# Linformer attention and a gelu MLP on one core: scores, sums and values in 64x32 tiles of TensorE, one round of sums per block, reciprocals copied to the heads' rows through DRAM

## Chip, cores and metric

One core of a Trainium2 chip. The metric is the time of one execution on the device in microseconds (us), the median of repeated executions. Most executions of a kernel agree within 0.3%.

## The reference

```python
# batch 8, heads 8, seq 1024, head_dim 64, k_proj 64; d_model 512, d_ff 2048; float32
k_proj = np.einsum('ks,bhsd->bhkd', E, k)
v_proj = np.einsum('ks,bhsd->bhkd', F, v)
scores = np.matmul(q, k_proj.transpose(0, 1, 3, 2)) / 8
attn = np.exp(scores - scores.max(-1, keepdims=True))
attn = attn / (attn.sum(-1, keepdims=True) + 1e-09)
x = np.matmul(attn, v_proj)            # -> [8192 tokens, 512]
h = x @ w_in                           # [8192, 2048]
out = (h / (1 + np.exp(-1.702 * h))) @ w_out
```

## The kernel before

The 8192 tokens are worked in 16 blocks of 512 (two blocks per batch). Each block j goes through ffn1 (16 slots of four matmuls) and ffn2 (eight slots O to O+7 of eight matmuls). The attention of later blocks is put between these slots with `at(block, slot, ...)`. A block's attention is scores, exp on ScalarE, then `norm`: sums of the exponentials over the 64 keys, values, reciprocal, product. A head has 64 keys and 64 columns, so each matmul is a 64x64 tile and four run in the array side by side.

```python
def four(outs, lhsTs, rhss):
    for i, ro in ((0, (LO, HI)), (1, (HI, LO))):
        for ri, r in zip((LO, HI), ro):
            nc.tensor.matmul(outs[i][r], lhsTs[i][ri], rhss[i][ri], start=True, stop=True)

def norm(h, u):                      # heads 4u .. 4u+3 of block h
    def go():
        e = [expT[h][:, 2 * u + i, :] for i in range(2)]
        d_ps = [ps_d.tile([P, TB], F32, name="d_ps") for _ in range(2)]
        four(d_ps, [ones, ones], e)                      # sums, already on the heads' rows
        n_ps = [ps_n.tile([P, TB], F32, name="n_ps") for _ in range(2)]
        four(n_ps, [vqs[h // NB2 % 2][:, 2 * u + i, :] for i in range(2)], e)
        for i in range(2):
            rden = att.tile([P, TB], F32, name="rden")
            nc.vector.reciprocal(rden, d_ps[i])
            nc.vector.tensor_tensor(x_of(h)[:, 2 * u + i, :], n_ps[i], rden, op=ALU.mult)
    return go
```

`ps_n` and `ps_d` have two PSUM buffers each, `ps_f` four: all eight banks are taken. Loads of q, k and v go on GpSimd's queue; outputs and the DMA transposes of q (`q_dma`) and of the projected k (in `kv_out`) go on the SP queue, in program order. In the schedule (cut):

```python
at(1, O + 7, q_dma(2))
at(2, 1, norm(3, 0)); at(2, 11, norm(3, 1))
at(2, 2, proj(2)); at(2, 3, kv_out(2))
for b in range(3, B):
    j = NB2 * b - 4
    at(j, O, q_dma(b)); at(j, O + 6, proj(b), kv_out(b))
at(2, O + 5, norm(4, 0)); at(3, 4, norm(4, 1))
for j in range(3, NBLK - 2):
    for u in range(2):
        at(j, O + 6 * u, scores(j + 3, u)); at(j, O + 6 * u, norm(j + 2, u))   # [cut]
```

The softmax here doesn't subtract the row's maximum and nothing guards it: scores larger than these inputs give would overflow.

Of the kernel before, what the change touches and what calls it, by code (L numbers as in the profile page):

```python
# [9 lines left out]
F32 = mybir.dt.float32  # L10
BF16 = mybir.dt.bfloat16
AF = mybir.ActivationFunctionType
ALU = mybir.AluOpType
# [4 lines left out]
def kernel(ctx, tc, q, k, v, E, F,  # L18
                                                     moe_w_in, moe_w_out, out):
    nc = tc.nc  # L20
    B, H, S, D = q.shape
    KP, _ = E.shape
    DM, DFF = moe_w_in.shape
    P = 128
    J = S // P
    NB2 = S // 512
    HP = H // 2
    KC = DM // P
    FC = DFF // P
    TB = 512  # L30
    JB = TB // P
    NBLK = B * S // TB
# [3 lines left out]
    consts = ctx.enter_context(tc.tile_pool(name="consts", bufs=1))  # L36
    ldpool = ctx.enter_context(tc.tile_pool(name="ldpool", bufs=1))
    att = ctx.enter_context(tc.tile_pool(name="att", bufs=2))
    work = ctx.enter_context(tc.tile_pool(name="work", bufs=2))
    ps_f = ctx.enter_context(tc.tile_pool(name="ps_f", bufs=4, space=PSUM))  # L40
    ps_d = ctx.enter_context(tc.tile_pool(name="ps_d", bufs=2, space=PSUM))
    ps_n = ctx.enter_context(tc.tile_pool(name="ps_n", bufs=2, space=PSUM))
    ctx.enter_context(tc.manual_schedule())


# [54 lines left out]
    LO, HI = slice(0, KP), slice(KP, P)  # L100
    X_LO, X_HI = slice(0, None, 3), slice(1, 3)
    kts = [consts.tile([P, HP, KP], BF16, name=f"kt{i}") for i in range(2)]
    vqs = [consts.tile([P, HP, D], BF16, name=f"vq{i}") for i in range(2)]
    zeros = consts.tile([P, TB], BF16)
    nc.vector.memset(zeros, 0.0)
    ones = consts.tile([P, D], BF16)
    nc.vector.memset(ones, 1.0)

    vxs = []
# [7 lines left out]
    def f_tile(shape, dt=F32):  # L117
        return ps_f.tile(shape, dt, name="f_ps")
# [15 lines left out]
    warm(4)  # L134


    kvps, kbs, qT, expT, xT = {}, {}, {}, {}, {}

    def proj(b):
        def go():  # L140
            kvps[b] = f_tile([P, H, D])
            for j in range(J):
                for e, r in enumerate((LO, HI)):
                    nc.tensor.matmul(kvps[b][r], eft[:, j, e * KP:(e + 1) * KP],  # L144
                                     (kt, vt)[e][b][:, :, j, :],
                                     start=(j == 0), stop=(j == J - 1))
        return go
# [21 lines left out]
    def v_out(b, v_ps, p0, n, cp=nc.vector.tensor_copy):  # L169
        if b < 2:  # L170
            if n == 1:
                for r, t in ((LO, p0 % 2), (HI, 1 - p0 % 2)):
                    cp(vxs[b][r, 2 * p0 + t, :D], v_ps[HI, t, :])
            else:
                vv = v_ps[HI].rearrange("k (u x) d -> k u x d", x=4)
                vx = vxs[b][:, 2 * p0:2 * (p0 + n), :D].rearrange("k (u x) d -> k u x d", x=4)
                for r, xs_ in ((LO, X_LO), (HI, X_HI)):
                    cp(vx[r, :, xs_], vv[:, :, xs_])
        if b > 0:
            vv = v_ps[HI].rearrange("k (u x) d -> k u x d", x=4)  # L180
            for r, xs_ in ((LO, X_LO), (HI, X_HI)):
                nc.vector.tensor_copy(vqs[b % 2][r].rearrange("k (u e) d -> k u e d", e=2), vv[:, :, xs_, :])

    def kv_out(b):
        def go():
            ps = kvps.pop(b)
            k_b = att.tile([KP, H, D], BF16, name="k_b")
            nc.vector.tensor_copy(k_b, ps[LO])  # L188
            if b > 1:
                nc.sync.dma_start_transpose(out=kts[b % 2], in_=k_b.rearrange("k h d -> k (h d)"))  # L190
            v_out(b, ps, 0, HP)
            kbs[b] = k_b
        return go
# [13 lines left out]
    def q_dma(b, j0=0, n=J):  # L207
        def go():
            if j0 == 0:
                qT[b] = att.tile([P, J, HP, P], BF16, name="qT")  # L210
            nc.sync.dma_start_transpose(out=qT[b][:, j0:j0 + n].rearrange("r j p s -> r (j p) s"),
                                        in_=qt[b][:, j0:j0 + n].rearrange("s j h d -> s (j h d)"))
        return go

    def four(outs, lhsTs, rhss):

        for i, ro in ((0, (LO, HI)), (1, (HI, LO))):
            for ri, r in zip((LO, HI), ro):
                nc.tensor.matmul(outs[i][r], lhsTs[i][ri], rhss[i][ri], start=True, stop=True)  # L219

    def scores(h, u, half=None):
        b, c = divmod(h, NB2)
        j0, n = (c * JB, JB) if half is None else (c * JB + half * JB // 2, JB // 2)
        ts = slice(j0 * P - c * TB, (j0 + n) * P - c * TB)

        def go():
            if h not in expT:
                expT[h] = att.tile([P, HP, TB], BF16, name="expT", bufs=3)
            s_ps = [f_tile([P, n * P]) for _ in range(2)]
            four(s_ps, [kts[b % 2][:, 2 * u + i, :] for i in range(2)],  # L230
                 [qT[b][:, j0:j0 + n, 2 * u + i, :] for i in range(2)])
            for i in range(2):
                nc.scalar.activation(expT[h][:, 2 * u + i, ts], s_ps[i], AF.Exp, scale=scale)  # L233
        return go
# [4 lines left out]
    def x_of(h):  # L239
        if h not in xT:  # L240
            xT[h] = att.tile([P, KC, TB], BF16, name="xT", bufs=3)
        return xT[h]

    def norm(h, u):
        def go():
            e = [expT[h][:, 2 * u + i, :] for i in range(2)]
            d_ps = [ps_d.tile([P, TB], F32, name="d_ps") for _ in range(2)]
            four(d_ps, [ones, ones], e)
            n_ps = [ps_n.tile([P, TB], F32, name="n_ps") for _ in range(2)]
            four(n_ps, [vqs[h // NB2 % 2][:, 2 * u + i, :] for i in range(2)], e)  # L250
            for i in range(2):
                rden = att.tile([P, TB], F32, name="rden")
                nc.vector.reciprocal(rden, d_ps[i])  # L253
                nc.vector.tensor_tensor(x_of(h)[:, 2 * u + i, :], n_ps[i], rden, op=ALU.mult)  # L254
        return go


# [18 lines left out]
    def x_tr(h, p, half):  # L276
        def go():
            x_sb = xs.pop((h, p, half)).rearrange("s (i t) d -> s i (t d)", i=2)
            n_ps = ps_n.tile([P, 2, P], BF16, name="n_ps")
            for i in range(2):  # L280
                nc.tensor.transpose(n_ps[:, i, :], x_sb[:, i, :], ident)  # L281
            cp = nc.scalar.copy if (h, half) == (0, 0) else nc.vector.tensor_copy
            cp(x_of(h)[:, p, half * TB // 2:(half + 1) * TB // 2], n_ps.rearrange("r i s -> r (i s)"))
        return go
# [53 lines left out]
    def at(j, slot, *fs):  # L338
        fill.setdefault((j, slot), []).extend(fs)

    O = FC
# [40 lines left out]
    for u in range(2):  # L382
        at(1, O + u, scores(2, u))
        at(1, O + 3 + u, scores(3, u))
        at(2, O + 2 * u, scores(4, u))
        at(2, O + 3 + 2 * u, scores(5, u))
    for p in range(HP):
        at(1, O + 2 + p, tok(2, p, 0), tok(2, p, 1))
        at(1, O + 3 + p, x_tr(2, p, 0), x_tr(2, p, 1))
    at(2, 1, norm(3, 0))  # L390
    at(2, 11, norm(3, 1))
    for j in (1, 2):
        at(j, O + 5, gelu_table)
    at(1, O + 7, q_dma(2))
    at(2, 2, proj(2))
    at(2, 3, kv_out(2))
    for b in range(3, B):
        j = NB2 * b - 4
        at(j, O, q_dma(b))
        at(j, O + 6, proj(b), kv_out(b))  # L400
    at(2, O + 5, norm(4, 0))
    at(3, 4, norm(4, 1))
    for j in range(3, NBLK - 2):
        for u in range(2):
            if j + 3 < NBLK:
                at(j, O + 6 * u, scores(j + 3, u))
            at(j, O + 6 * u, norm(j + 2, u))
        if j + 3 < NBLK:
            at(j, O + 7, gelu_table)

# [47 lines left out]
```

## Time and profile before

| | before |
|---|---|
| time, median of 3 (range) | 517.87 us (517.22 to 519.39) |
| span of the profile, granted TensorE clock | 515.9 us, 0.999 |
| busy: TensorE, VectorE, ScalarE | 98%, 48%, 51% |
| TensorE waits past 60 us | one, 1.5 us, for v of batch 3 |

Engines in the lines below: PE is TensorE, PEld its weight loads, DVE VectorE, ACT ScalarE, POOL GpSimd, SP the queue of the sync engine. The granted clock is the share of the full TensorE clock that the throttle allowed. In the chain of work that ended last a line is start (us), length (us), what. The prediction shows the lines of this kernel that carry the argument.

### The profile page before, as it was taken

To read this page: it belongs to the slowest core of one execution; us is meant where nothing else is said; L and a number is where in the kernel's file an instruction comes from. 1 tells how busy PE (TensorE), PEld (TensorE's weight loads), DVE (VectorE), ACT (ScalarE), POOL (GpSimd) and SP (SyncE) were. 2 spreads that over 40 slices of the span, in tenths; PEclk is the share of its full clock that TensorE was granted. 3 is DMA by queue.
4 is the path that set the end of the run, shared out by engine and by line. 5 is a ranking of instruction groups with operands and counts; after the bars stand their busy time and mean duration, and the time that the engine had idled before them with its cause. 6 is when DMAs were issued, how large, how long until landed. Compare 5 with 4: busy or idle time off the path is not lost.

```text
span 515.9 us, 6686 instructions
## 1 busy us (share of the span) xinstructions
PE 505.4 (98%) x2824; PEld 232.3 (45%) x2824; DVE 248.4 (48%) x227; ACT 262.6 (51%) x439; POOL 77.3 (15%) x96
## 2 busy tenths in 40 slices
PE   7899999998999999999999999999999999999997
PEld 3584445443444444444444444444444444444444
DVE  2633124757665663726747264665637366560000
ACT  1575564563637456372655627375472737344351
POOL 7442051062400051000510024000000000000000
PEclk9999999999999999999999999999999999999999
DMA  9999999999986059350993209960200102010102
GB/s 169 197 203 207 217 128 148 206 144 165 208 103 164 1 80 209 74 133 0 169 164 113 51 9 210 115 163 1 88 0 1 81 1 82 1 82 1 81 1 81
DMA packets 118110, 54.83 MB, mean 106 GB/s; under 512 B 91840, under 2 KB 115648, under 8 KB 116160
## 3 DMA queue, kind: packets, MB, share of 16 engines
q0 software_dynamic: 84384, 29.37, 51.1%
q1 hardware_dynamic: 33616, 24.78, 17.4%
q8 instruction: 22, 0.36, 0.3%
q10 hardware_dynamic: 80, 0.26, 0.2%
q14 instruction: 8, 0.07, 0.0%
HBM read 59.24 MB, written 16.78 MB: 147 GB/s over the span
## 4 chain that ended last, share of the span: by engine, by line
PE 90%; DMA 6%; POOL 1%; DVE 1%; ACT 1%; issue 0%; POOLq 0%; DVEq 0%; ACTq 0%
PE f_ps L327 40%; PE f_ps L295 40%; DMA qT<-q_sb 3%; PE f_ps L144 2%; DMA v_sb<-in_v_dram 2%; PE f_ps L219 2%; POOL q_sb L63 1%; PE d_ps L219 1%; DMA ef_f<-in_E_dram 1%; PE n_ps L219 1%; PE f_ps L319 1%; PE n_ps L281 1%; PE f_ps L123 1%; PE f_ps L152 1%; PE d_ps L266 0%
## 5 line engine op out<-in xcount | busy, mean ns | idle before, releaser
L253 DVE RECIPROCAL rden<-d_ps 128x512 f32<-128x512 f32 x52 | 174.4, 3353 | 135.1 <-PE d_ps L219 135.0
L327 PE MATMUL f_ps<-w_out_sb,gT 128*128 128x512 bf16 x1008 | 227.2, 379 | 0.0
L295 PE MATMUL f_ps<-xT,w_in_sb 128*128 128x512 bf16 (+1 forms) x1088 | 226.7, 367 | 0.2
L298 ACT ACTIVATE gT<-f_ps 128x512 bf16<-128x512 f32 (+1 forms) x268 | 151.3, 575 | 63.0 <-PE f_ps L295 62.0
L295 PEld LDWEIGHTS <-w_in_sb 128*128 128x128 bf16 x1088 | 105.3, 98 | 115.8 <-issue 2.3
L327 PEld LDWEIGHTS <-gT 128*128 128x128 bf16 x1008 | 95.7, 98 | 120.5 <-issue 11.5
L330 ACT COPY o_sb<-f_ps 128x512 f32<-128x512 f32 x63 | 36.9, 585 | 134.6 <-PE f_ps L327 124.8
L63 POOL DMA_DIRECT2D q_sb<-in_q_dram x56 | 49.0, 901 | 53.0 <-DMA k_sb<-in_k_dram 31.5
L233 ACT ACTIVATE expT<-f_ps 128x512 bf16<-128x512 f32 (+1 forms) x68 | 35.2, 572 | 36.3 <-PE f_ps L219 36.2
L254 DVE TENSOR_TENSOR xT<-n_ps,rden 128x512 bf16<-128x512 f32 x52 | 36.0, 692 | 5.4
L57 POOL DMA_DIRECT2D k_sb<-in_k_dram x9 | 7.8, 864 | 176.2 <-PE f_ps L144 174.6
L321 DVE COPY o_sb<-f_ps 128x256 f32<-128x256 f32 x1 | 0.4, 425 | 49.2 <-PE f_ps L319 49.2
L188 DVE CAST k_b<-f_ps 64x512 bf16<-64x512 f32 x7 | 4.8, 680 | 30.1 <-PE f_ps L144 30.1
L233 ACT ACT_TABLE_LOAD x13 | 16.7, 1283 | 4.7 <-PE f_ps L219 4.5
L237 ACT ACT_TABLE_LOAD x14 | 18.0, 1283 | 0.3
L144 PE MATMUL f_ps<-v_sb,eft 128*64 128x512 bf16 x56 | 13.4, 381 | 1.5 <-DMA v_sb<-in_v_dram 1.5
L219 PE MATMUL f_ps<-qT,kt 64*64 64x512 bf16 (+1 forms) x136 | 13.8, 386 | 0.4 <-ACT expT L233 0.4
L144 PE MATMUL f_ps<-k_sb,eft 128*64 128x512 bf16 x56 | 13.6, 382 | 0.0
L271 DVE RECIPROCAL rd<-d_ps 128x4 f32<-128x4 f32 x22 | 4.0, 184 | 17.4 <-PE d_ps L266 17.4
L219 PEld LDWEIGHTS <-kt 64*64 64x64 bf16 x136 | 4.0, 103 | 14.3 <-issue 14.2
L219 PE MATMUL d_ps<-expT,ones 64*64 64x512 bf16 x104 | 10.2, 381 | 0.0
L219 PE MATMUL n_ps<-expT,vq 64*64 64x512 bf16 x104 | 10.0, 376 | 0.0
(55 smaller groups left out, 121.8 us busy)
## 6 DMA issues: line engine op xcount, KB each, us to landing
out_dram<-o_sb SPq DMA_DIRECT2D x15, 1024.0 KB, 4.5
k_sb<-in_k_dram POOLq DMA_DIRECT2D x7, 1024.0 KB, 13.1
v_sb<-in_v_dram POOLq DMA_DIRECT2D x7, 1024.0 KB, 10.8
q_sb<-in_q_dram POOLq DMA_DIRECT2D x56, 128.0 KB, 13.0
w_in_sb<-in_moe_w_in_dram POOLq DMA_DIRECT2D x8, 256.0 KB, 12.7
w_out_sb<-in_moe_w_out_dram POOLq DMA_DIRECT2D x4, 512.0 KB, 14.7
k_sb<-in_k_dram POOLq DMA_DIRECT2D x2, 512.0 KB, 7.4
out_dram<-o_sb SPq DMA_DIRECT2D x3, 256.0 KB, 2.0
```

Of the source, the lines that this page charges most:

```text
L57: nc.gpsimd.dma_start(out=dst[b][:, h:h + n, js:js + jn], in_=sv[:, h:h + n, js:js + jn])
L63: nc.gpsimd.dma_start(out=qt[b][:, j], in_=qv[:, j])
L144: nc.tensor.matmul(kvps[b][r], eft[:, j, e * KP:(e + 1) * KP], (kt, vt)[e][b][:, :, j, :], start=(j == 0), stop=(j == J - 1))
L219: nc.tensor.matmul(outs[i][r], lhsTs[i][ri], rhss[i][ri], start=True, stop=True)
L233: nc.scalar.activation(expT[h][:, 2 * u + i, ts], s_ps[i], AF.Exp, scale=scale)
L237: nc.scalar.preload_act_table(AF.Gelu_apprx_sigmoid)
L253: nc.vector.reciprocal(rden, d_ps[i])
L254: nc.vector.tensor_tensor(x_of(h)[:, 2 * u + i, :], n_ps[i], rden, op=ALU.mult)
L295: nc.tensor.matmul(h_ps, w_in_sb[:, kc, fc * P:(fc + 1) * P], xT[j][:, kc, ts], start=(kc == 0), stop=(kc == KC - 1))
L298: nc.scalar.activation(gts[j][:, fc, ts], h_ps, AF.Gelu_apprx_sigmoid)
L327: nc.tensor.matmul(o_ps[n], gts[j][:, fc, n * P:(n + 1) * P], w_out_sb[:, fc, :], start=(fc == 0), stop=(fc == FC - 1))
L330: nc.scalar.copy(osb[j][:, n, :], o_ps.pop(n))
```

## The change

The intent: a head's sum is the same for all of its columns, so 32 identical rows per head are enough, and then one round of eight 64x32 tiles gives the sums of all eight heads where two rounds did. So that no switch of tile mode stands between scores, sums and values, all three go to 64x32. The reciprocals then lie on other rows than the values: one row per head is written to DRAM, and read back spread over the head's 64 rows. With that the reciprocals halve as well.

```diff
+    dram = ctx.enter_context(tc.tile_pool(name="dram", bufs=2, space=bass.MemoryType.DRAM))
-    ones = consts.tile([P, D], BF16)
+    ones = consts.tile([P, 32], BF16)
-    def four(outs, lhsTs, rhss):
+    def eight(outs, lhsTs, rhss):
         for i, ro in ((0, (LO, HI)), (1, (HI, LO))):
-            for ri, r in zip((LO, HI), ro):
-                nc.tensor.matmul(outs[i][r], lhsTs[i][ri], rhss[i][ri], start=True, stop=True)
+            for c in range(0, KP, 32):
+                for ri, r in zip((LO, HI), ro):
+                    nc.tensor.matmul(outs[i][r.start + c:r.start + c + 32], lhsTs[i][ri, c:c + 32], rhss[i][ri],
+                                     start=True, stop=True)
-    def norm(h, u):
[cut]
+    def sums(h):
+        def go():
             d_ps = [ps_d.tile([P, TB], F32, name="d_ps") for _ in range(2)]
+            for p in range(HP):
+                for e in range(2):
+                    r = HI if (p + e) % 2 else LO
+                    nc.tensor.matmul(d_ps[e][32 * p:32 * p + 32], ones[r], expT[h][r, p, :], start=True, stop=True)
+            rbc[h] = att.tile([P, HP, TB], F32, name="rbc")
+            rdr[h] = dram.tile([2, HP, TB], F32, name="rdr")
+            for e, r in enumerate((LO, HI)):
+                rden = att.tile([P, TB], F32, name="rden")
+                nc.vector.reciprocal(rden, d_ps[e])
+                nc.sync.dma_start(out=rdr[h][e], in_=rden[0:P:32, :])
+                nc.sync.dma_start(out=rbc[h][r], in_=rdr[h][e:e + 1].to_broadcast([D, HP, TB]))
+    def values(h, u):
[cut: n_ps by eight(), product with rbc[h] instead of rden]
-        at(2, O + 2 * u, scores(4, u))
+        at(2, O + 2 * u, scores(4, u), values(3, u))
-    at(2, 1, norm(3, 0))
-    at(2, 11, norm(3, 1))
-    at(2, 2, proj(2))
-    at(2, 3, kv_out(2))
+    at(2, 2, proj(2), kv_out(2), sums(3))
+    at(2, O + 5, sums(4))
+    at(2, O, q_dma(3))
+    at(3, 4, proj(3), kv_out(3), values(4, 0))
-    for b in range(3, B):
+    for b in range(4, B):
         j = NB2 * b - 4
-        at(j, O, q_dma(b))
         at(j, O + 6, proj(b), kv_out(b))
+        at(j, O + 7, q_dma(b))
[cut: in block j >= 3, values(j+1, 1) and sums(j+2) at O, values(j+2, 0) at O+6]
```

More of the change, by code (lines that the diff above doesn't have):

```diff
@@ L134 @@
     warm(4)
-    kvps, kbs, qT, expT, xT = {}, {}, {}, {}, {}
+    kvps, kbs, qT, expT, xT, rbc, rdr = {}, {}, {}, {}, {}, {}, {}
     def proj(b):
@@ L229, in go @@
             s_ps = [f_tile([P, n * P]) for _ in range(2)]
-            four(s_ps, [kts[b % 2][:, 2 * u + i, :] for i in range(2)],
+            eight(s_ps, [kts[b % 2][:, 2 * u + i, :] for i in range(2)],
                  [qT[b][:, j0:j0 + n, 2 * u + i, :] for i in range(2)])
@@ L242, in x_of @@
         return xT[h]
-    def norm(h, u):
+    def sums(h):
         def go():
-            e = [expT[h][:, 2 * u + i, :] for i in range(2)]
             d_ps = [ps_d.tile([P, TB], F32, name="d_ps") for _ in range(2)]
-            four(d_ps, [ones, ones], e)
+            for p in range(HP):
[9 more added lines that the diff above has]
+                nc.sync.dma_start(out=rbc[h][r], in_=rdr[h][e:e + 1].to_broadcast([D, HP, TB]))
+        return go
+    def values(h, u):
+        def go():
             n_ps = [ps_n.tile([P, TB], F32, name="n_ps") for _ in range(2)]
-            four(n_ps, [vqs[h // NB2 % 2][:, 2 * u + i, :] for i in range(2)], e)
+            eight(n_ps, [vqs[h // NB2 % 2][:, 2 * u + i, :] for i in range(2)],
+                  [expT[h][:, 2 * u + i, :] for i in range(2)])
             for i in range(2):
-                rden = att.tile([P, TB], F32, name="rden")
-                nc.vector.reciprocal(rden, d_ps[i])
-                nc.vector.tensor_tensor(x_of(h)[:, 2 * u + i, :], n_ps[i], rden, op=ALU.mult)
+                nc.vector.tensor_tensor(x_of(h)[:, 2 * u + i, :], n_ps[i], rbc[h][:, 2 * u + i, :], op=ALU.mult)
         return go
@@ L394 @@
     at(1, O + 7, q_dma(2))
-    at(2, 2, proj(2))
-    at(2, 3, kv_out(2))
-    for b in range(3, B):
+    at(2, 2, proj(2), kv_out(2), sums(3))
[3 more added lines that the diff above has]
+    for b in range(4, B):
         j = NB2 * b - 4
-        at(j, O, q_dma(b))
         at(j, O + 6, proj(b), kv_out(b))
-    at(2, O + 5, norm(4, 0))
-    at(3, 4, norm(4, 1))
-    for j in range(3, NBLK - 2):
+        at(j, O + 7, q_dma(b))
+    for j in range(3, NBLK - 1):
         for u in range(2):
@@ L406 @@
                 at(j, O + 6 * u, scores(j + 3, u))
-            at(j, O + 6 * u, norm(j + 2, u))
+        at(j, O, values(j + 1, 1))
+        if j + 2 < NBLK:
+            at(j, O, sums(j + 2))
+            at(j, O + 6, values(j + 2, 0))
         if j + 3 < NBLK:
```

## The prediction

> **What bounds the kernel now.** I read the page's busy shares first, then the chain of work that ended last, then that chain and the timeline inside one steady block, and last the timeline around the one place where TensorE waits. The page:
>
> ```profile
> PE 505.4 (98%) x2824; PEld 232.3 (45%) x2824; DVE 248.4 (48%) x227; ACT 262.6 (51%) x439; POOL 77.3 (15%) x96
> ...
> PE 90%; DMA 6%; POOL 1%; DVE 1%; ACT 1%; issue 0%; POOLq 0%; DVEq 0%; ACTq 0%
> ...
> L253 DVE RECIPROCAL rden<-d_ps 128x512 f32<-128x512 f32 x52 | 174.4, 3353 | 135.1 <-PE d_ps L219 135.0
> ```
>
> TensorE is the chain; VectorE is half idle. The 52 reciprocals of 3.353 us look expensive, but VectorE idles 135 us ahead of them, waiting for TensorE, and in the list of waits TensorE never waits for a reciprocal. Halving them is worth nothing by itself; what counts is TensorE time. The chain in a steady stretch of 29 us (start, us, what):
>
> ```profile
> 261.95 1.73 PE f_ps L327 x8
> 263.68 0.34 PE f_ps L219 x4
> 264.02 0.22 PE d_ps L219 x4
> 264.24 0.22 PE n_ps L219 x4
> 264.45 10.46 PE f_ps L327 x48
> ```
>
> Eight full matmuls take 1.73 us, so one takes 0.216. A round of four 64x64 matmuls (scores f_ps, sums d_ps, values n_ps) also takes 0.22: the four run side by side. The visit to 64x64 mode costs 0.12 going in (0.34 less 0.22) and 0.10 coming out (10.46 less 48 x 0.216 = 10.37). So a round is worth 0.216 us and a separate visit 0.22.
>
> The only wait of TensorE after the first 60 us, and what lies ahead of it (timeline; the chain view; groups of waits):
>
> ```profile
> 90.62 7.14 SPq L211 DMA_TRANSPOSE qT<-q_sb  x1
> ...
> 100.21 1.29 SPq L190 DMA_TRANSPOSE kt<-k_b  x1
> ...
> 111.92 0.41 PE L219 MATMUL f_ps<-qT,kt 64*64 64x512 bf16 x4
> ...
> 116.03 7.92 SPq L211 DMA_TRANSPOSE qT<-q_sb  x1
> ...
> 122.53 0.38 PE L144 MATMUL f_ps<-v_sb,eft 128*64 128x512 bf16 x1 [1.53 <-DMA v_sb<-in_v_dram]
> ```
> ```profile
> 90.62 13.32 DMA qT<-q_sb
> ...
> 111.42 11.07 DMA v_sb<-in_v_dram
> ```
>
> The projection of batch 3 in block 2 stands 1.53 us for v_sb. Here the DMA queues are crowded: the transpose of q for batch 2 keeps the SP queue issuing for 7.14 us and lands only after 13.3 us, at 103.9.
>
> **What the Trainium skill says.** "TensorEngine Tiling (Array Packing)", Key Properties: tiles work independently, 64x32 is a legal mode with eight of them, and changing the mode drains the array. The trace agrees for 64x64: 0.22 us per visit. "TensorE: Matmul & The Clock Gate", Part 3: tiles in one array start about 4 ns apart. In the trace four starts take 0.41 us with 400 ns each, so 3 ns apart. For eight tiles of 32 columns no run here shows it yet. "DMA: Bandwidth & Descriptors", Queues, rings and completion order: each DMA engine takes a queue's descriptors in ring order. The k transpose issued at 100.21 landed after 6.7 us, at 106.9, about 3 us behind q's 103.9, though the fastest k transpose of the run takes 2.3; that fits, or is plain contention. "TensorE: Matmul & The Clock Gate", HAM oscillation: an idle gap above some 3 us can halve the clock. No gap that long is in this trace; the granted clock is 0.999.
>
> **The change part by part.**
>
> 1. Scores and values: eight 64x32 matmuls for four 64x64. If eight run abreast, a round stays 0.216 us: no gain, no loss. Reason to do it: sums can be 64x32 without a switch of mode between the parts.
>
> 2. Sums: 32 columns for each head, so one round serves all eight heads, where two did. 52 reciprocals at 4 per block are 13 blocks: 13 x 0.216 = **2.8 us** off TensorE, on the chain.
>
> 3. Visits to another mode. Gone: the visits of norm(3,0) and norm(3,1) in block 2 and the one of proj(3) in block 2, six switches. New: sums(3) on the heels of proj(2), and proj(3) ahead of values(4,0), one more switch each; the visit of values(15,1) in block 14, two. Net two switches: **0.2 us** off.
>
> 4. proj(3) moves from near the end of block 2 into the first third of block 3. In before, TensorE has from 124.4 one part of ffn2 (1.7) and five slots of ffn1 (5 x 0.864 = 4.3) before that place, so it would be reached near 130, when v_sb (122.5) has long landed: the wait of **1.5 us** goes.
>
> 5. VectorE: 26 reciprocals less, 26 x 3.353 = 87 us less busy; off the chain. The 52 products stay at 0.69.
>
> 6. New transfers: per block two writes of 8 KB to DRAM and two reads of 512 KB spread over 64 rows, on the SP queue, each read waiting for its write. In before an output of 128 KB lands in 1.8 us, 256 KB in 2.0, 1 MB in 4.5, and in 9.5 at 129.0 beside loads. My estimate from these: write 1.8; read 3 to 4 in quiet, 4 to 6 beside loads. In a steady block, from the start of the group after the first part of ffn2: two products to 2.0 us, first reciprocal 5.4, second 8.7, second write 10.6, second read 14. values(j+2,0) runs on TensorE at 6 x 1.73 + 0.6 = 11 us, so its product on VectorE stands some 3 us; but n_ps is next needed at 29 us and xT a block later. Hidden. The later q transpose (after the seventh part) has some 16 us until the scores that need it and lands in 8.6 to 13.3: hidden, by a few us.
>
> Sum with all transfers hidden: 517.9 - 2.8 - 0.2 - 1.5 = **513.4 us**.
>
> **The rivals.**
>
> A. *Block 2 gets a new wait: TensorE stands for n_ps until the reciprocals of block 3 have come round through DRAM.* sums(3) run at about 93.9. kv_out(2) goes first on VectorE, so the reciprocals end at about 98.9 and 102.2. The SP queue is busy with q's transpose to 97.8, then k's to 99.1, then the first write. It stands behind transposes that land at 104 to 106, so it lands at about 104 to 107; first read, beside the loads of q_sb from 104.5, 4 to 6 us: 108 to 113; second write just behind it, second read 112 to 119. Then the product, 0.7. TensorE reaches values(3,1) at about 111.5 (before: scores there at 111.92, less a round and a switch or so) and n_ps has two buffers, both held by values(3,0). The wait is 1 to 8 us, middle 4.5. If it comes it eats points 2 to 4, as they come to 4.5 together. Above 3 us the clock may drop, for 1 to 2 us more. For: crowded queues in just this place. Against: if the small write overtakes the transposes (landing near 101) the second read lands near 110 and nothing waits. I give a wait above 2 us 60%. Time with it: 516 to 520.
>
> B. *The k transpose of batch 3 comes late for scores(6,0) in block 3.* It now queues on SP behind q's transpose, four transfers of sums(4) and an output of 1 MB; issued near 133, landing near 141 if it takes 7.7 like most, needed at about 140 when A does not come, 145 when it does. So 0 to 2 us, in place of A, not on top.
>
> C. *Eight tiles of 32 columns do not run abreast*, for the streams or the instruction rate: 16 instructions per 0.216 us where 8 were. If a round took double: per block ten slots of 0.216 for six, 13 x 4 x 0.216 = 11 us more, minus the 1.7 of points 3 and 4: 527. Against: the 4 tiles issue in 10 ns, and the steady groups follow long stretches at 0.108 us per instruction, in which a queue can fill. 6%.
>
> D. *Nothing is slower, and less DMA pressure helps:* not seen; the change adds 13 x 1 MB of reads. At best 512.5.
>
> **Range and chances.** About 0.4 x 514.0 (hidden, with some of B) + 0.54 x 517 (A, mild to middle) + 0.06 x 526 (C, partly) = 516.3; I say **516.0 us**. Range **512.5 to 520.5**: low end the full sum, high end A at its largest. Two per cent is 10.4 us: faster needs under 507.5, more than twice what TensorE can give up: 0.01. Slower needs over 528: C in full, or A with a clock drop: 0.04. Within: **0.95**.
>
> **What would show each step.** (1) A scores round of eight stays at 0.22 in the chain, and sums have 8 matmuls per block. (2) d_ps in the chain falls from 1.0% to about 0.5%. (3) TensorE's wait for v_sb is gone from the list of waits. (4) 26 reciprocals, VectorE near 161 us busy. (5) For A: between 111 and 120 us TensorE waits for the product of block 3, whose VectorE idle time ends with rbc landing; for B: TensorE near 140 waits for kt. (6) Past 150 us a block is shorter by 0.2 us and no more. The prediction is wrong if steady blocks show waits of TensorE (for rbc, qT or kt), if rounds of eight take over 0.3 us, or if the wait in block 2 exceeds 8 us.

## The result, and the profile after

The changed kernel took 526.6 us (median of 4, 525.47 to 527.6) against 518.61 (517.22 to 519.39) for the kernel before beside it: a ratio of 1.0156, 95% interval 1.0119 to 1.0194. Here and below a ratio is the mean time of one kernel's fast runs over that of the other's of the same rounds, so not quite the ratio of the medians quoted. The span of the profile grew from 515.9 to 523.9 us, by 8.0.

The page of the changed kernel:

```profile
PE 504.6 (96%) x3064; PEld 231.2 (44%) x3064; DVE 158.3 (30%) x201; ACT 262.5 (50%) x439; POOL 77.3 (15%) x96
...
PE 75%; DMA 13%; issue 7%; POOL 2%; DVE 1%; ACT 0%; SPq 0%; POOLq 0%; DVEq 0%
...
L261 DVE RECIPROCAL rden<-d_ps 128x512 f32<-128x512 f32 x26 | 85.3, 3322 | 7.1 <-PE d_ps L256 7.0
```

VectorE lost 90 us of work and DMA came into the chain. A steady stretch shows that the part meant to pay does pay. This is its chain, where L222 is scores (f_ps) or values (n_ps), and d_ps is the one round of sums:

```profile
180.63 0.34 PE f_ps L222 x8
180.97 0.21 PE n_ps L222 x8
181.19 0.22 PE d_ps L256 x8
181.40 10.47 PE f_ps L345 x48
...
223.22 0.22 PE n_ps L222 x8
```

Eight tiles cost 0.21 to 0.22 us, as four did, and the group at the second place (223.22 here) is scores and values alone. Two blocks took 60.61 us before (the ffn2 piece of 154.47 to that of 215.08) and take 60.18 now (163.26 to 223.44): 0.215 per block, the one round.

The loss lies in block 2. The chain there, then the timeline of TensorE and VectorE at the wait, then the granted clock (in the last fence the columns after the window are busy time of PE, PEld, DVE, ACT, POOL; then clock, DMA share, GB/s):

```profile
98.75 7.16 DMA rdr<-rden
105.92 0.49 SPq L263
106.50 6.31 DMA rdr<-rden
112.83 7.45 DMA rbc<-rdr
120.40 0.70 DVE xT L272
122.36 3.26 PE f_ps L345 x8
```
```profile
111.28 0.41 PE L222 MATMUL f_ps<-qT,kt 64*32 64x512 bf16 x8
...
120.40 2.70 DVE L272 TENSOR_TENSOR xT<-n_ps,rbc 128x512 bf16<-128x512 f32 x4 [18.47 <-DMA rbc<-rdr]
121.14 1.21 PE L222 MATMUL n_ps<-expT,vq 64*32 64x512 bf16 x8 [9.46 <-DVE xT L272]
...
125.55 0.41 PE L222 MATMUL f_ps<-qT,kt 64*32 64x512 bf16 x8
```
```profile
110.00:120.00 10.00, 1.69 (x15) 0.51 (x13) 0.00 (x0) 1.59 (x4) 0.80 (x1) 0.75 1.66 196
120.00:130.00 10.00, 8.86 (x56) 3.00 (x55) 2.58 (x4) 2.02 (x4) 0.00 (x0) 0.74 0.92 147
```

Read from the end: values(3,1) wanted n_ps at 111.7; both buffers were held by values(3,0); its product waited for rbc; rbc's second read landed after 7.45 us, the write it waited for after 6.31, and the first write, with 8 KB, after 7.16. The second write was also issued late, at 106.50: its reciprocal was done at 101.9, but the first read stands ahead of it in the program, and the SP queue stood until 105.92 for the write that this read needs. TensorE stood for 9.46 us, and the eight full matmuls after it took 3.26 us instead of 1.83: the clock was at 0.50 from 115 to 125 us.

The balance of the 8.0 us, by the times at which both traces reach the same work:

| stretch | after less before |
|---|---|
| to scores(4,1) in block 2 (111.28 against 111.92) | -0.64 |
| from there to scores(5,0) (125.55 against 114.09): the wait of 9.46, the round of values(3,1), its second product, the slow clock | +12.10 |
| to the first ffn2 part of block 3 (149.74 against 140.73): no wait for v_sb (1.9 with what follows it, see e6), two rounds and one mode switch less | -2.45 |
| from there to the end: ten rounds less, one visit more, a wait of 1.0 for qT at 332 | -1.0 |

### The profile page after: what moved, and what is told of

Same layout as the page of the kernel before. It is cut to its first block, busy times and chain, and to the rows that moved or that the text cites. A ratio compares the mean times of both kernels' runs of the same rounds, so it can differ in the third digit from the quotient of the medians.

```text
span 523.9 us, 7197 instructions
## 1 busy us (share of the span) xinstructions
PE 504.6 (96%) x3064; PEld 231.2 (44%) x3064; DVE 158.3 (30%) x201; ACT 262.5 (50%) x439; POOL 77.3 (15%) x96
## 4 chain that ended last, share of the span: by engine, by line
PE 75%; DMA 13%; issue 7%; POOL 2%; DVE 1%; ACT 0%; SPq 0%; POOLq 0%; DVEq 0%
PE f_ps L345 36%; PE f_ps L313 32%; DMA qT<-q_sb 6%; DMA w_in_sb<-in_moe_w_in_dram 3%; DMA rdr<-rden 3%; PE f_ps L145 2%; PE f_ps L222 2%; DMA rbc<-rdr 1%; POOL q_sb L64 1%; PE n_ps L222 1%; DMA k_sb<-in_k_dram 1%; DVE rden L261 1%; POOL v_sb L58 1%; PE n_ps L299 0%; PE d_ps L284 0%
## 5 line engine op out<-in xcount | busy, mean ns | idle before, releaser
L313 PEld LDWEIGHTS <-w_in_sb 128*128 128x128 bf16 x1088 | 105.2, 98 | 115.9 <-issue 1.1
L345 PEld LDWEIGHTS <-gT 128*128 128x128 bf16 x1008 | 96.0, 98 | 121.7 <-issue 13.3
L272 DVE TENSOR_TENSOR xT<-n_ps,rbc 128x512 bf16<-128x512 f32 x52 | 33.5, 686 | 231.6 <-PE n_ps L222 122.1
L261 DVE RECIPROCAL rden<-d_ps 128x512 f32<-128x512 f32 x26 | 85.3, 3322 | 7.1 <-PE d_ps L256 7.0
L222 PE MATMUL n_ps<-expT,vq 64*32 64x512 bf16 x208 | 11.3, 386 | 9.5 <-DVE xT L272 9.5
L222 PE MATMUL f_ps<-qT,kt 64*32 64x512 bf16 (+1 forms) x272 | 13.8, 374 | 1.5 <-DMA qT<-q_sb 1.0
L222 PEld LDWEIGHTS <-kt 64*32 64x32 bf16 x272 | 4.0, 88 | 15.5 <-issue 14.4
L291 DVE TENSOR_TENSOR x_sb<-d_ps,rd 128x256 bf16<-128x256 f32 x22 | 9.3, 425 | 0.8
L124 PE MATMUL f_ps<-zeros 128*128 128x512 bf16 x24 | 8.3, 492 | 1.2 <-DVE zeros L106 1.2
(55 smaller groups left out, 111.5 us busy)
```

What stands on the lines that cost most here:

```text
L222: nc.tensor.matmul(outs[i][r.start + c:r.start + c + 32], lhsTs[i][ri, c:c + 32], rhss[i][ri], start=True, stop=True)
L261: nc.vector.reciprocal(rden, d_ps[e])
L313: nc.tensor.matmul(h_ps, w_in_sb[:, kc, fc * P:(fc + 1) * P], xT[j][:, kc, ts], start=(kc == 0), stop=(kc == KC - 1))
L345: nc.tensor.matmul(o_ps[n], gts[j][:, fc, n * P:(n + 1) * P], w_out_sb[:, fc, :], start=(fc == 0), stop=(fc == FC - 1))
```

## The experiments

The standing theory after the result: the kernel gains what was predicted and loses it to one wait in block 2 and the slow clock after it. The rivals: the 64x32 tiles cost something; the copies cost something in every block; another transfer is late as well. Eleven kernels were run, all correct. The ratios are to the kernel before in the same rounds.

### e1_tiles_only: the tile form alone

```diff
-    def four(outs, lhsTs, rhss):     # in the kernel before, for scores, sums and values
+    def eight(outs, lhsTs, rhss):    # as in the change; sums still in two rounds of norm()
```

> The kernel before with every group of four 64x64 matmuls cut into eight of 64x32 (sums still in two rounds, no DMA, no schedule change). Theory (eight run abreast, a round stays 0.216 us): within 0.5 us of the kernel before, about 518.6. Rival (eight cost more, by streams or instruction rate): each of 6 rounds per block longer, at a quarter of a round more 13 x 6 x 0.05 = 4 us, so 522 or more.

Measured: 518.88 us (6 runs) against 517.69, ratio 1.0019 (0.9994 to 1.0045); span 515.6 against 515.9. Its chain:

```profile
263.48 0.34 PE f_ps L221 x8
263.82 0.21 PE d_ps L221 x8
264.03 0.22 PE n_ps L221 x8
264.25 10.47 PE f_ps L330 x48
```

The form costs nothing that these runs show: the same 0.34, 0.22, 0.22 as with four tiles. (The times alone would leave up to 2.3 us open, the end of the interval; the trace does not.) Rival C of the prediction is out.

### e2_old_block3: block 3 without the detour

```diff
-    at(2, O + 2 * u, scores(4, u), values(3, u))
+    at(2, O + 2 * u, scores(4, u))
-    at(2, 2, proj(2), kv_out(2), sums(3))
+    at(2, 1, norm(3, 0))             # sums in two rounds of 64x32 tiles, reciprocals in place
+    at(2, 2, proj(2), kv_out(2))
+    at(2, 11, norm(3, 1))
[cut: norm() put back, ones 64 wide again]
```

> The changed kernel, with block 3 alone as before: its own two rounds of sums at each half, early in block 2, reciprocals used in place, no DRAM. Theory (the whole loss is the one wait of 9.5 us in block 2 and the slow clock after it, some 2.4 us): 526.6 - 9.5 - 2.4 + 0.6 for the rounds and visits that come back = about 515.3, below the kernel before by 3 us; no wait above 2 us near 111. Rival (the copies of the later blocks or the tile form cost too): 517 or more, with new waits of TensorE past 130 us.

Measured: 522.0 us (6 runs), ratio 1.008 (1.0058 to 1.0103). The expectation missed by 7 us: the theory of one wait falls. The wait for n_ps was gone, but another had come, 30 us later, at scores(6,0). Waits of TensorE, the chain, and the SP queue:

```profile
PE f_ps L222 <- DMA kt<-k_b: 5.4, 1, 5.4
```
```profile
134.17 11.46 DMA kt<-k_b
145.67 0.63 PE f_ps L222 x8
...
147.16 11.97 PE f_ps L358 x48
```
```profile
132.87 0.46 SPq L263 DMA_DIRECT2D rbc<-rdr  x1
133.43 0.64 SPq L365 DMA_DIRECT2D out_dram<-o_sb  x1
134.17 1.21 SPq L191 DMA_TRANSPOSE kt<-k_b  x1
```

The k transpose of batch 3 was issued only after the last read of block 4's copies and the 1 MB output, and landed after 11.46 us (7.7 is the median before). This is rival B of the prediction, which said that it comes in place of A; its size had been put at 0 to 2 us and was 5.4. The clock fell again (0.50 from 145 to 150 us): 48 matmuls took 11.97 us instead of 10.47.

### e3_busy_wait: the wait without the idleness

```diff
-    at(2, O + 2 * u, scores(4, u), values(3, u))             # for u = 1
+    at(2, O + 2 * u, scores(4, u), lambda: warm(44), values(3, u))
```

> The changed kernel, with 44 matmuls of zeros (44 x 0.216 = 9.5 us) ahead of values(3,1), so that TensorE works through the wait. Theory (the idle time halves the clock, which costs 2.0 to 2.4 us after it): about 524.3, granted clock back to 0.999. Rival (matmuls after the wait are slow for another reason, such as weight loads): 526.6 or more.

Measured: 524.65 us (4 runs), ratio 1.0130 (1.0108 to 1.0152), where the changed kernel has 1.0156 (1.0119 to 1.0194). The intervals overlap, so the times alone do not show the gain; the trace does:

```profile
124.12 1.90 PE L345 MATMUL f_ps<-w_out_sb,gT 128*128 128x512 bf16 x8
```
```profile
120.00:130.00 10.00, 8.73 (x58) 3.50 (x64) 2.48 (x4) 1.62 (x4) 0.00 (x0) 1.00 0.94 176
```

The granted clock was 1.00 in both ten-microsecond windows from 110 to 130, and the eight matmuls after the wait took 1.90 us in the timeline, where the changed kernel shows 3.33 there. From the start of the first product to scores(5,0) it took 3.51 us (122.44 to 125.95), in the changed kernel 5.15 (120.40 to 125.55). So the slow clock costs some 1.6 us, less than the 2.0 to 2.4 expected, and the idleness brings it on. The span is only 0.5 us shorter than that of the changed kernel, as the copies landed 2.0 us later in this traced run. The slow matmuls were not a cost of weight loads.

### e4_loads_late: the same copies without loads beside them (a diagnosis)

```diff
+    def gated():
+        g = work.tile([P, 1], BF16, name="gate")
+        nc.gpsimd.tensor_copy(g, xT[3][:, 1, :1])   # waits for the first product of block 3
+        load(3)                                     # and no load(3) at the start of block 2
-    at(2, O, q_dma(3))
+    at(2, O + 1, gated, q_dma(3))
```

> The changed kernel, with the loads of batch 3 held back until the first product of block 3 is done (a tiny copy on GpSimd waits for it). A diagnosis, not a candidate: v of batch 3 will come late for its projection. Theory 1 (the copies are slow because loads share the DMA engines): the first write, issued near 99, lands in about 3 us instead of 7.2, the second read in 3 to 4 instead of 7.5, and the wait for n_ps near 111 shrinks from 9.5 us to under 2. Theory 2 (they stand behind the q and k transposes in the SP queue, whatever the loads do): the first write still takes 6 us or more and the wait stays above 5.

Measured: 532.98 us (one run), as v and k of batch 3 now came too late (waits of 8.3 and 6.0 us). What it was for is in the SP queue; each read is issued when its write has landed:

```profile
98.80 0.61 SPq L262 DMA_DIRECT2D rdr<-rden  x1
100.55 0.48 SPq L263 DMA_DIRECT2D rbc<-rdr  x1
102.01 0.51 SPq L262 DMA_DIRECT2D rdr<-rden  x1
105.18 0.46 SPq L263 DMA_DIRECT2D rbc<-rdr  x1
```

The first write took 1.7 us instead of 7.2, the second 3.2 instead of 6.3, and the product began at 109.89, so the second read took under 4.7 instead of 7.45. There was no wait for n_ps. The q and k transposes stood ahead in the queue just as before. So the loads are what makes the four transfers long (theory 1), the transposes ahead of them perhaps included; the order of the queue alone is not enough.

### e5_q_early: the q transposes of batches 4 to 7 back in their old place

```diff
+        at(j, O, q_dma(b))
         at(j, O + 6, proj(b), kv_out(b))
-        at(j, O + 7, q_dma(b))
```

> The changed kernel, with the q transposes of batches 4 to 7 back ahead of the sums of the same block, as in the kernel before. Theory (the wait for qT of 1 us and whatever stands near 275 and 333 us comes of the late place): 1 to 1.5 us less, 525.3, no wait for qT. Rival (ahead of the sums, the transposes delay the copies of sums so that values wait): 526.6 or more, with new waits for n_ps.

Measured: 526.77 us (4 runs), ratio 1.018 (1.016 to 1.020). In the trace the wait for qT is gone and the span is 522.9 where the changed kernel has 523.9, as expected; the wait for n_ps is still 9.4. But the timed runs do not show the 1 us: three of four took 526.7 to 526.9, and 1.018 is not below 1.0156. The trace is of the fourth, of 524.68, so its span proves no gain either. Inconclusive in time; only the missing wait speaks for it.

### e6_proj3_moved: the moved projection alone

```diff
-        at(j, O + 6, proj(b), kv_out(b))            # for b = 3, in the kernel before
-    at(3, 4, norm(4, 1))
+    at(3, 4, proj(3), kv_out(3), norm(4, 1))
```

> The kernel before, with only the projection of batch 3 and its copies moved from block 2 to block 3. Theory (the wait for v_sb of 1.5 us goes and one visit to another mode): about 518.6 - 1.5 - 0.1 = 517.0. Rival (the k transpose that hangs on it then comes late for scores(6,0)): a wait for kt near 140 us takes its place, 518 to 520.

Measured: 515.52 us (6 runs) against 517.69, ratio 0.9959 (0.9943 to 0.9976). TensorE no longer waits for v_sb, and not for kt either. A change of two lines, without tiles, sums or DRAM, is worth 2.2 us; the prediction had 1.5 for the wait and 0.1 for one mode switch. The wait cost more than itself: with it the projection took 3.76 us in before (120.60 to 124.36), without it 1.85 here (126.37 to 128.22), so 1.9.

### e7_old_3_and_4: copies only from block 5 on

```diff
     [as e2_old_block3, and]
-    at(2, O + 5, sums(4))
+    at(2, O + 5, norm(4, 0))
-    at(3, 4, proj(3), kv_out(3), values(4, 0))
+    at(3, 4, proj(3), kv_out(3), norm(4, 1))
+        at(j, O, q_dma(b))                          # instead of O + 7
-        at(j, O, values(j + 1, 1))
+        if j > 3:
+            at(j, O, values(j + 1, 1))
[cut]
```

> The changed kernel, with blocks 3 and 4 by their own sums as before and the q transposes early; only blocks 5 to 15 take their reciprocals through DRAM. Theory (all losses sit in the crowded stretch to 150 us; from block 5 on the copies are hidden and each block saves one round of 0.216 us): 515.5 of the kernel before with proj(3) moved, less 11 x 0.216 = 2.4: 513.2, no wait of TensorE over 0.5 us past 20 us. Rival (the copies cost TensorE time in steady blocks too): 515.5 or more.

Measured: 513.24 us (6 runs, 512.88 to 514.59) against 517.3, ratio 0.9924 (0.9908 to 0.9939). This beats both kernels. In the list of waits nothing stops TensorE for more than 0.5 us past 20 us (32 of the 1008 matmul records of ffn2 are missing from this trace, and leave gaps of 0.16 that are no waits). But some 2.2 us of its 4.1 are those of e6, whose moved projection it contains. The rest is the change itself: its span, 511.4, is 2.1 us below e6's 513.5, and eleven rounds less (2.4) with one visit more (0.2) are 2.2. Eleven blocks still take their reciprocals through DRAM, so the copies cost nothing that shows where they have room. In a quiet steady block the read that waits for the first write is issued 1.7 us after it:

```profile
174.55 0.51 SPq L262 DMA_DIRECT2D rdr<-rden  x1
176.25 0.48 SPq L263 DMA_DIRECT2D rbc<-rdr  x1
```

### e8_k3_on_pe: e2 with k of batch 3 transposed on TensorE

```diff
     [as e2_old_block3, and]
-            if b > 1:
+            if b > 1 and b != 3:
                 nc.sync.dma_start_transpose(out=kts[b % 2], ...)
-    at(3, 4, proj(3), kv_out(3), values(4, 0))
+    at(3, 4, proj(3), kv_out(3))
+    at(3, 6, lambda: k_tr(3, kbs[3], 0), values(4, 0))
```

> The kernel of e2_old_block3 (block 3 by its own sums), with k of batch 3 transposed on TensorE instead of by DMA, so that it no longer stands in the SP queue behind the copies of block 4. Theory (its wait of 5.4 us for kt and the slow clock after it, some 2 us, are all that it lost): 522.0 - 5.4 - 2.0 + 0.4 for four transposes = 515.0; a wait for qT of 1 us stays. Rival (something else in that stretch is late as well, such as rbc of block 4 for n_ps): above 517.

Measured: 516.66 us (4 runs), ratio 0.9987 (0.9970 to 1.0005), so 0.93% below e2. The wait for kt and its slow clock are gone. It is 1.7 us above the expectation: waits of 1.4 us for qT and 0.8 for n_ps are left, the last because block 4's copies are still only just in time. So the late k transpose was the cause of most of what e2 lost.

### e9_q2_ahead: the q transpose of batch 2 out of the way

```diff
-    at(1, O + 7, q_dma(2))
+    at(1, 15, q_dma(2))
```

> The changed kernel, with only the q transpose of batch 2 put ahead of the output of block 1 in the SP queue, so that it is issued near 85, when its loads have landed, not near 90.6, and is out of the way when the copies of block 3 begin near 98.8. Theory 1 (the loads alone make the copies slow): as at 156.6, where a first write beside loads took 4.8 us and a second 5.5: second write landed near 109, second read 115 to 117, a wait of 4 to 6 us, 521 to 523. Theory 2 (it takes transposes and loads together): writes in 2 to 3 us, wait under 2 us, 515 to 517.

Measured: 525.31 us (4 runs), ratio 1.0144 (1.0116 to 1.0172). The transpose was issued at 85.3. The copies:

```profile
99.13 0.61 SPq L262 DMA_DIRECT2D rdr<-rden  x1
103.82 0.49 SPq L263 DMA_DIRECT2D rbc<-rdr  x1
104.40 0.51 SPq L262 DMA_DIRECT2D rdr<-rden  x1
111.60 0.47 SPq L263 DMA_DIRECT2D rbc<-rdr  x1
```

The first write fell from 7.2 to 4.7 us, as theory 1 had it, but the second rose to 7.2 and the second read took 7.0; the wait is 7.6 us where theory 1 said 4 to 6 and theory 2 under 2. But the run changed more than the transpose. GpSimd loads q of the next batch as soon as the transpose has released q_sb: it issued these loads from 95.2 us and v's at 106.3, where the changed kernel did from 102.9 and at 109.9. The loads so came onto the second write: from 103 to 106 us the DMA share column shows 2.06, in the changed kernel 1.22. That fits theory 1 and is the likely reason why the second write was no faster, but no run moves the transpose with the loads held back. With e4 the verdict stands that the loads make the copies slow; what the transpose ahead of them adds is not shown.

### e10_one_hop: SBUF to SBUF, without DRAM

```diff
-                nc.sync.dma_start(out=rdr[h][e], in_=rden[0:P:32, :])
-                nc.sync.dma_start(out=rbc[h][r], in_=rdr[h][e:e + 1].to_broadcast([D, HP, TB]))
+                for p in range(HP):
+                    nc.sync.dma_start(out=rbc[h][r.start:r.start + D // 2, p, :], in_=rden[32 * p:32 * p + D // 2, :])
+                    nc.sync.dma_start(out=rbc[h][r.start + D // 2:r.stop, p, :], in_=rden[32 * p:32 * p + D // 2, :])
```

> The changed kernel, with the copies made straight from SBUF to SBUF (each head's 32 equal rows to its first and second 32 rows, 16 copies of 64 KB per block on the SP queue), so no write to DRAM and no read that waits for it. Theory (the wait comes of four transfers one after another, of which the two writes took 7.2 and 6.3 us): the copies of the second half are issued by 106 and landed by 112, the wait in block 2 falls from 9.5 us to under 2, 515 to 518, unless kt of batch 3 is late in its place. Rival (the 1 MB of bytes in the crowded stretch is what takes the time, whatever the hops): the wait stays above 5 us, 522 or more.

Measured: 525.5 us (4 runs), ratio 1.0152 (1.0129 to 1.0175). Waits of TensorE:

```profile
PE n_ps L222 <- DVE xT L272: 4.0, 2, 3.0
PE f_ps L222 <- DMA kt<-k_b: 3.7, 1, 3.7
```

Between the two expectations. The wait for n_ps fell from 9.5 to 4.0 us. But the edit changed two things: the writes are gone, and a product now waits for its own four copies, not for one read of a whole half. The first two products of values(3,0), which free n_ps, had their copies by 115.9; the last copy landed near 118.7 (the fourth product stood for it until 118.77), where the last read of the changed kernel landed at 120.3. So the copies as a whole ended only 1.6 us earlier, and most of the shorter wait comes of the smaller pieces. That the bytes in the crowded stretch make the rest is likely, not shown. But 16 issues of 0.6 us per block hold the SP queue for 11 us (128.5 to 139.7 for block 4), and the k transpose of batch 3 behind them came late in turn. The time did not move.

### e11_hop_q_ahead: one hop and all q transposes early

```diff
     [as e10_one_hop, and q_dma(2) at (1, 15), q_dma(b) at (j, O) for b >= 4]
```

> The changed kernel with the copies from SBUF to SBUF and all q transposes early (that of batch 2 ahead of the output, those of batches 4 to 7 ahead of the sums). A try for the best version. If nothing waits: the 511.4 span of e7_old_3_and_4 less two more rounds and a visit, 0.6: a time of 512.6. If the 16 issues per block on the SP queue delay other transfers (kt of batch 3 or q): 514 to 518.

Measured: 522.15 us (4 runs), ratio 1.0086 (1.0057 to 1.0115). Waits of 2.3 us for n_ps and 3.3 for kt are left. A miss as a candidate: giving the copies a shorter path, in smaller pieces, does not bring out what e7_old_3_and_4 gets by not making them in the crowded stretch.

## Why the prediction was wrong

*The bound, the round and the visit* (TensorE on the chain; 0.216 us a round, 0.22 a visit): right. e1 shows a round of eight at the cost of a round of four, and the steady blocks are shorter by 0.215 us, where the prediction said 0.2.

*Points 1 to 5 of the sum*: right in size. Reciprocals fell to 26 and VectorE's busy time to 158 us (predicted 161). The wait for v_sb went, worth 2.2 us with one mode switch by e6 (predicted 1.6). The full sum of 513.4 with all transfers hidden is what e7 reached, 513.24, without the copies of blocks 3 and 4 (its own expectation, 513.2, counted their two rounds as not saved). That it is the same number is in part luck: the kernel before took 517.3 in the rounds of e7, not 517.9, and the gain was 4.1 us, not 4.5.

*Rival A*: the failed step is the size of this term, "The wait is 1 to 8 us, middle 4.5", and the weight that it got. The mechanism was the right one, down to the buffer and the place: TensorE at 111.7 for n_ps (predicted about 111.5), held by a product that waits for rbc. Of its links, the first write landed at 105.9 (predicted 104 to 107) and the second at 112.8 (108 to 113, "just behind" the first read; in fact 6.3 us of its own). The second read took 7.45 us, not 4 to 6, and landed at 120.3, not 112 to 119. The middle value had taken each link at its middle; the links share one cause, the loads (e4), so they came out long together. The wait was 9.46 us. Nor does its own sum fit its range: 513.4 and the largest wait, 8, are 521.4, above the high end of 520.5.

*The slow clock*: named in rival A ("for 1 to 2 us more"), e3 measures 1.6 us, but the range left it out: its high end is "A at its largest" without the clock. 513.4 + 9.5 + 1.6 is already 524.5, and 1.0 for qT makes 525.5; the kernel before was 0.7 us slower in the rounds of the result than in those of the prediction, which makes 526.2, near the 526.6 measured.

*Point 6, the late q transpose* ("hidden, by a few us"): wrong for one batch. It was allowed 8.6 to 13.3 us, as in the traces of before; one took 15.09 beside a k load, and the room was 14.3 us (317.9 to 332.2), not some 16, so TensorE waited 1.0 us.

*Rival B* ("0 to 2 us, in place of A, not on top"): the "in place of" is right, e2 shows it, but it measured 5.4 us plus the clock. The prediction had taken the landing time of before, 7.7, for a transpose that now stands behind 1 MB of output and a read of 0.5 MB; it took 11.46. Hence "about 0.4 x 514.0" for the case without A was too low too: with A gone, B gives 522.0.

What stays open: how much the transposes ahead of the copies cost once the loads are apart (e9 moved both), and whether e5's 1 us is real in time. An obvious variant was not run: both writes of a block issued ahead of both reads, so that the second write, ready at 101.9, does not stand until 106.5.

## What to carry to other kernels

A detour through DRAM is free where nobody waits for it, and the same code is a loss in the one stretch where the DMA engines are full: place such a copy by the busiest block, not by the typical one, and here simply leave it out there (e7, 0.76% faster than before, where the full change is 1.6% slower; about half of that gain is the moved projection, which needs no copies at all). When several links of a chain are slow for one reason, add them at their slow ends, and add the clock that TensorE loses after standing. When one wait is taken away, run the kernel again before believing the sum: the next late transfer in the same queue may take its place, as in e2 and e10. And when an experiment frees a buffer earlier, look at which loads then start earlier, as in e9.

## What the Trainium skill lacked or had wrong

- "TensorEngine Tiling (Array Packing)", Key Properties: says that a change of mode drains the array, without a size. Here a visit to 64x64 or 64x32 mode costs 0.22 us in all (0.12 in, 0.10 out). It has no measured time for eight 64x32 tiles either: a round with 512 columns took 0.22 us, as with four tiles (e1). (The prediction puts the mode 64x32 with its eight tiles under Key Properties too; on the page it stands under Available Configurations.)
- "DMA: Bandwidth & Descriptors", Anatomy of one DMA (SWDGE path): gives a fixed cost near 2 us plus bytes over the rate, for transfers issued by GpSimd. The page has no such sum for the SP queue, which issued the copies here: 8 KB landed in 1.7 us in quiet (e7). Nor has it a landing time beside other traffic: the same 8 KB took 4.7 to 7.2 us beside loads and transposes, and 512 KB some 7.0 to 7.45.
- The same page, Queues, rings and completion order: "completion is **not FIFO per issuing engine**" is borne out. In the changed kernel the k transpose was issued at 96.81, ahead of the first write at 98.75, but the weight load that reads it stood for it until 107.16, while the write had landed by 105.92. The prediction had placed the write behind the transposes by ring order, and named overtaking only as what would spare the wait.
- "TensorE: Matmul & The Clock Gate", HAM oscillation: an idle gap over some 3.4 us takes the clock to half. Agrees in the changed kernel: some 3.3 us into the wait of 9.46 us the granted clock went to 0.50, the loss was 1.6 us, and dummy matmuls avoided it (e3). But the figure is no sharp limit here: after a wait of 3.33 us in e11 and waits of 2.97 and 0.98 us in e10 the clock fell to 0.50, both times when TensorE already worked again, and after a wait of 3.70 us in e10, ended at 150.12, it stayed at 1.00.
